# A decode layer on one core: wo loaded with eight rows to a partition, another selection of the attention output, and W_down's third quarter loaded in three parts

## The chip, the cores and the metric

The kernel runs on one core of a Trainium2 chip. The core has five engines with programs of their own: TensorE (PE; PEld is its loading of weights), VectorE (DVE), ScalarE (ACT), GpSimd (POOL) and SyncE (SP). They meet through semaphores. Data come from the chip's memory (HBM) by DMA: an engine, here nearly always SP, issues a transfer, and 16 DMA engines carry it out in the order of SP's queue. The metric is the device time of one execution in microseconds (us), lower is better. The kernel before takes 384.69 us, the median of three runs (384.29 to 384.77).

## The reference

One decode step (four sequences, one token each, model width 576) of a transformer layer: normalization, attention over a window of a cache, projection, residual, normalization, a gated feed-forward block, residual. All tensors are bf16.

```python
def _A_ref(x, k_cache, v_cache, wq, wo):       # 32 query heads, 16 kv heads, head size 128
    W = min(4096, max(256, Sk // 4))           # Sk = 16384: the last 4096 positions
    q = (x @ wq).reshape(B, Sq, Hq, Dh).transpose(0, 2, 1, 3)
    k = jnp.repeat(k_cache[:, :, Sk - W:, :], rep, axis=1)   # rep = 2
    v = jnp.repeat(v_cache[:, :, Sk - W:, :], rep, axis=1)
    scores = jnp.einsum("bhqd,bhkd->bhqk", q, k) * (Dh ** -0.5)
    o = jnp.einsum("bhqk,bhkd->bhqd", _softmax(scores), v)
    return o.transpose(0, 2, 1, 3).reshape(B, Sq, Hq * Dh) @ wo      # wo: 4096 x 576

def _B_ref(x, W_gate, W_up, W_down):           # 576 x 4608, 576 x 4608, 4608 x 576
    gate = jnp.einsum("bsd,df->bsf", x, W_gate)
    up = jnp.einsum("bsd,df->bsf", x, W_up)
    gate = gate * (gate > 0)
    return jnp.einsum("bsf,fd->bsd", gate * up, W_down)

h = x + _A_ref(_layernorm(x), A_k_cache, A_v_cache, A_wq, A_wo)
h2 = h + _B_ref(_layernorm(h), B_W_gate, B_W_up, B_W_down)
```

Nearly all bytes are the cache's windows: 64 loads of 2 MB, and some 25 MB of weights.

## The kernel before

The program is written once per engine (`prog_sync`, `prog_pool`, `prog_act`, `prog_dve`, `prog_pe`). A small class, `Sched`, counts what each engine has done: an operation may carry a name, and another that lists the name in `deps` waits for its engine's counter. So the order on each engine is the order in which the code is written, and a wait holds back all that stands behind it on the same engine. Every DMA has a semaphore of its own kind; `land(name)` is the wait for its landing.

*Memory and the load queue.* One buffer, `pool`, has eight slots of 2 MB: four for K, four for V. `add` (lines 195 to 206) puts a transfer on a list and notes which earlier users of those bytes must be done. SP walks through that list (`prog_sync`, line 263): wq, then K and V in turn (a "duo" is two kv heads of one sequence, 4096 positions each), then, into slots that have come free, the four loads of wo (`("wo", g)`, g = 0 to 3), W_gate and W_up (`wg0`, `wu0`, `wg1`, `wu1` of 256 rows each, then `wg4`, `wu4` of the last 64), and W_down (`("wd", k)`). W_down's 4608 rows are 36 chunks of 128 rows; it is loaded as `WD` says (line 247): three quarters of nine chunks each, then 3, 3, 2 and 1 chunks. In a quarter, each partition holds nine rows that are neighbours in memory. The W_down loads overwrite the bytes of wo, so the first of them waits for `ATTN`, the last matmul of the output projection.

*Attention.* Per duo VectorE transposes K (`tr`), TensorE multiplies by the query (`qk`), and per batch of four duos VectorE takes maxima, ScalarE the exponentials, VectorE transposes the probabilities, TensorE multiplies by V (`pv`). `ext` and `norm` bring the result to `oT_all`: 128 partitions (a head's 128 features) by 32 heads by 4 sequences.

*The output projection (lines 587 to 603).* The product with wo sums over 4096 rows (head and feature). A load of wo covers 1024 rows, which is eight heads. Before the change a partition holds two pieces of four neighbouring rows (4608 bytes each): row 512 q + 4 p + e of the load lies in partition p. So the attention output must be rearranged to fit: for each e and each head's place h4 in a group of four, one matmul with a strided piece of the identity picks the features 4 k + e of eight heads and puts them on 32 partitions (16 matmuls, 32 columns each, `OSEL`); VectorE copies the result as bf16 to `oX` (`D_OX`, line 464). Then 160 matmuls, each with a 128 x 128 (or 128 x 64) piece of wo as the weights and four columns of `oX`, add up into one PSUM bank (`WOB`).

*After it.* VectorE adds the residual (`H1`, `H2`), TensorE sums for mean and variance (`STAT`), VectorE and ScalarE normalize (`S1` to `N2`), and TensorE runs gate and up: 40 matmuls for each of four 128-feature slices, each slice's weights waited for, and then those of the last 64 features. ScalarE and VectorE form max(gate, 0) x up and transpose it (`HHT`), and TensorE multiplies by W_down: per chunk two matmuls of 288 columns, one for each half of the output, on different partitions. Each transfer of W_down is waited for before its first chunk. ScalarE and VectorE copy the two halves to `out_sb`, and SP stores it.

Of the kernel before, what the change touches and what calls it, by code (L numbers as in the profile page):

```python
# [21 lines left out]
FC = F // 128  # L22
DC = 5
NDUO = B * KVH // 2
NB = 4
NBATCH = NDUO // NB
# [7 lines left out]
ROW = 4608  # L34
GU0 = 24064
NWO = 4
# [66 lines left out]
def bass_sequential_preLN__sliding_block_cached__glu_gated_reglu__decode_kernel(  # L103
# [12 lines left out]
    with ExitStack() as es:  # L116
        cnt = [0]

        def sb(name, shape, dt):
            return es.enter_context(nc.sbuf_tensor(name, shape, dt))  # L120

        pool = sb("pool", [128, (NKS + NVS) * DUO], BF16)
        kT = sb("kT", [128, NKT, DUO // 4], FP32)
        ident_b = sb("ident_b", [128, 128], BF16)
# [11 lines left out]
        x4 = sb("x4", [64, B], BF16)  # L136
        dup = sb("dup", [64, 128], BF16)
        par = sb("par", [128, 2], FP32)
        oX = sb("oX", [128, 4, H // 4, B], BF16)
        xT = sb("xT", [128, DC, B], FP32)  # L140
        qT_sb = sb("qT_sb", [128, H * B], BF16)
        qrep = sb("qrep", [128, 4, H * B], BF16)
# [12 lines left out]
        P = sb("P", [128, T * 32], FP32)  # L155
        probT = sb("probT", [128, T, 32], FP32)
# [4 lines left out]
        oT_all = sb("oT_all", [128, H, B], BF16)  # L161
# [6 lines left out]
        gate_sb = P[:, 0:NG * JW].rearrange("p (g j f) -> p g j f", g=NG, j=JJ)  # L168
        hh = P[:, NG * JW:NG * JW + NG * JW // 2].bitcast(BF16).rearrange("p (g j f) -> p g j f", g=NG, j=JJ)
        hhT = probT[:, 0:FC // 2, :].bitcast(BF16).rearrange("p f b -> p (f b)")[:, 0:FC * 32].rearrange("p (f b) -> p f b", b=32)  # L170
        out_sb = sb("out_sb", [B, D], BF16)

        sc = es.enter_context(nc.psum_tensor("sc", [128, 2048], FP32))
        pb = [sc[:, i * 512:(i + 1) * 512] for i in range(4)]
        pb += [es.enter_context(nc.psum_tensor(f"pb{i}", [128, 512], FP32))[:, :] for i in range(4, 8)]
        PVB, OB, QB, QR, TPB = 4, 6, 6, 3, 7
        OSB, WOB, STB, SUB, DNB = 0, 1, 2, 5, 4


        GUB = ((0, 3, 6), (7, 1, 2))  # L180
# [7 lines left out]
        S = Sched()  # L188
# [4 lines left out]
        at = {}  # L193
# [30 lines left out]
        for c in range(2):  # L224
            add(("wq", c), f"wq{c}", NKS * DUO + 2 * c * HQ, 2 * HQ, "QMM",
                lambda e, o, c=c: e.dma_start(out=o, in_=A_wq[c * 256:(c + 1) * 256, :].rearrange("(p u) n -> p (u n)", u=2)))
# [6 lines left out]
                add_V(m - VLEAD)  # L233
        for g in range(NWO):
            add(("wo", g), f"wo{g}", g * ROW, ROW, "ATTN",
                lambda e, o, g=g: e.dma_start(out=o.rearrange("p (q x) -> p q x", q=2),
                                              in_=A_wo[g * 1024:(g + 1) * 1024, :].rearrange("(q p e) n -> p q (e n)", q=2, e=4)))
        for c in range(2):
            for k, (kind, W) in enumerate((("wg", B_W_gate), ("wu", B_W_up))):
                add((kind, c), f"{kind}{c}", GU0 + (4 * c + 2 * k) * ROW, 2 * F, None,  # L240
                    lambda e, o, c=c, W=W: e.dma_start(out=o, in_=W[c * 256:(c + 1) * 256, :].rearrange("(p u) n -> p (u n)", u=2)))
        for u, (kind, W) in enumerate((("wg", B_W_gate), ("wu", B_W_up))):
            add((kind, 4), f"{kind}4", GU0 + 8 * ROW + u * HALF, HALF, None,
                lambda e, o, W=W: e.dma_start(out=o, in_=W[512:576, :].rearrange("r (u n) -> (r u) n", u=2)))

        wd_sb = pool[:, 0:FC * D].rearrange("p (g x) -> p g x", g=NG)
        WD = [(0, 9), (9, 18), (18, 27), (27, 30), (30, 33), (33, 35), (35, 36)]
        for k, (f0, f1) in enumerate(WD):
            g0, j0 = divmod(f0, JJ)
            g1, nj = (f1 // JJ, JJ) if f1 - f0 >= JJ else (g0 + 1, f1 - f0)  # L250
# [2 lines left out]
                                  out=wd_sb[:, g0:g1, j0 * D:(j0 + nj) * D],  # L253
                                  in_=B_W_down[g0 * 128 * JJ:g1 * 128 * JJ, :].rearrange("(g p j) n -> p g (j n)", p=128, j=JJ)[:, :, j0 * D:(j0 + nj) * D])))

        def feat(c):
            return slice(c // 2 * 256 + c % 2, c // 2 * 256 + c % 2 + 255, 2) if c < 4 else slice(512, D)
# [104 lines left out]
        def prog_dve(S):  # L362
            v = "vector"
            S.op(v, lambda e: e.tensor_scalar(out=st1[:, 2:3], in0=st1[:, 0:1], scalar1=1.0 / D, scalar2=None, op0=ALU.mult),
                 deps=["A_SUM"], name="D1")
# [4 lines left out]
                 deps=["D3"], name="D_VARC")  # L370
            for ce in range(4):
                S.op(v, lambda e, ce=ce: e.tensor_copy(  # L372
                    out=sel[:, ce, :, :],
                    in_=bass.AP(tensor=ident_b, offset=64 * (ce // 2) + ce % 2, ap=[[128, 128], [0, 4], [2, 32]])),
                    deps=["IDB"], name=f"SEL{ce}")
            S.op(v, lambda e: e.tensor_copy(out=dup[:, :].rearrange("p (r u) -> p r u", u=2),
                                            in_=bass.AP(tensor=ident_b, offset=0, ap=[[128, 64], [1, 64], [0, 2]])), name="DUP")
            S.op(v, lambda e: e.tensor_reduce(out=par[:, :], in_=ident_b[:, :].rearrange("p (r u) -> p u r", u=2), axis=AX.X, op=ALU.add),
                 name="PAR2")
            for x in range(2):  # L380
# [3 lines left out]
                                              axis=AX.X, op=ALU.add), name="M0")  # L384
            S.op(v, lambda e: e.tensor_scalar(out=mask[:, 1, :], in0=mask[:, 0, :], scalar1=2 * BIG, scalar2=-BIG, op0=ALU.mult, op1=ALU.add),
                 deps=["M0"], name="M1")
            S.op(v, lambda e: e.tensor_scalar(out=mask[:, 2, :], in0=mask[:, 0, :], scalar1=-2 * BIG, scalar2=BIG, op0=ALU.mult, op1=ALU.add),
                 name="M2")
            for u in range(2):
                S.op(v, lambda e, u=u: e.tensor_reduce(out=rsel[:, u:u + 1], in_=mask[:, 1, :].rearrange("p (r s h) -> p s r h", s=2, h=2)[:, u, :, :],  # L390
                                                       axis=AX.XY, op=ALU.max), deps=["M1"] if u == 0 else [], name=f"RSEL{u}")
# [4 lines left out]
                 deps=["TP1"], name="D_XNT0")  # L396
# [3 lines left out]
            for u in range(2):  # L400
                S.op(v, lambda e, u=u: e.tensor_scalar(out=xn4[:, u, :], in0=pb[STB][:, 0:B], scalar1=par[:, u:u + 1], scalar2=None, op0=ALU.mult),
                     deps=["XDUP", "PAR2"], name=f"XN4{u}")
# [41 lines left out]
            for i in range(2 * NDUO):  # L444
                tr(i)
                if i == 0:
# [3 lines left out]
                                                    in_=bass.AP(tensor=ident_f, offset=0, ap=[[128, 128], [4, 4], [32, NB], [1, 4]])),  # L450
                         deps=["IDF"], name="SELT")
                n, pos = divmod(i, 2 * NB)
# [5 lines left out]
                if i >= 29 and (i - 29) % KVH == 0:  # L458
                    norm((i - 29) // KVH)
            trp(NBATCH - 1)  # L460
            for b in range(B):
                if 29 + KVH * b >= 2 * NDUO:
                    norm(b)
            S.op(v, lambda e: e.tensor_copy(out=oX[:, :, :, :].rearrange("p e q b -> p (e q b)"), in_=pb[OSB][:, 0:H * B]),
                 deps=["OSEL"], name="D_OX")

            S.op(v, lambda e: e.tensor_tensor(out=R_sb[:, 0, 0:4, :], in0=pb[WOB][:, 0:16].rearrange("p (c b) -> p c b", b=B),
                                              in1=xT[:, 0:4, :], op=ALU.add), deps=["ATTN", "R0", "D_XT"], name="H1")
            S.op(v, lambda e: e.tensor_tensor(out=R_sb[0:64, 0, 4, :], in0=pb[WOB][0:64, 16:20], in1=xT[0:64, 4, :], op=ALU.add), name="H2")
            S.op(v, lambda e: e.tensor_tensor(out=R_sb[:, 1, :, :], in0=R_sb[:, 0, :, :], in1=R_sb[:, 0, :, :], op=ALU.mult),  # L470
                 deps=["H2"], name="D_R")
            S.op(v, lambda e: e.tensor_reduce(out=st2[:, 0:8], in_=pb[SUB][:, 320:360].rearrange("p (s c b) -> p s b c", s=2, c=DC, b=B),
                                              axis=AX.X, op=ALU.add), deps=["STAT"], name="S1")
# [5 lines left out]
                 deps=["S4"], name="D_VARC2")  # L479
# [21 lines left out]
        def prog_pe(S):  # L501
            t = "tensor"

            def mm(o, l, r, start, stop, deps=(), name=None, skip=False):
                S.op(t, lambda e: e.matmul(o, lhsT=l, rhs=r, start=start, stop=stop, skip_group_check=skip),  # L505
                     deps=deps, name=name, signal=name is not None)
# [16 lines left out]
            s = at[("wq", 4)]  # L523
# [60 lines left out]
                    pv(i - PVLAG)  # L584
            ext(NBATCH - 1)

            for e_ in range(4):
                for h4 in range(4):
                    mm(pb[OSB][32 * h4:32 * h4 + 32, e_ * 32:(e_ + 1) * 32], ident_b[:, e_:128:4],
                       oT_all[:, :, :].rearrange("p (q h) b -> p h q b", h=4)[:, h4, :, :], True, True,  # L590
                       deps=[("NORM", b) for b in range(B)] if e_ == 0 and h4 == 0 else [],
                       name="OSEL" if e_ == 3 and h4 == 3 else None)
            for g in range(NWO):
                wv = pool[:, at[("wo", g)]:at[("wo", g)] + ROW].rearrange("p (q e n) -> p q e n", q=2, e=4)
                deps = [land(("wo", g))] + (["D_OX"] if g == 0 else [])
                for n in range(DC):
                    w = 128 if n < 4 else 64
                    for q in range(2):
                        for e_ in range(4):
                            last = g == NWO - 1 and n == DC - 1 and q == 1 and e_ == 3  # L600
                            mm(pb[WOB][0:w, n * B:(n + 1) * B], wv[:, q, e_, feat(n)], oX[:, e_, 2 * g + q, :],
                               g == 0 and n == 0 and q == 0 and e_ == 0, last, deps=deps, name="ATTN" if last else None, skip=True)
                            deps = []
            mm(pb[SUB][:, 320:360], ones_f[:, :], R_sb[:, :, :, :], True, True, deps=["D_R"], name="STAT")
            mm(pb[SUB][:, 400:400 + B], dup[:, :], hnT[0:64, 4, 0:B], True, True, deps=["N2"], name="HDUP")

# [90 lines left out]
```

## Time and profile before

| | |
|---|---|
| median of three runs | 384.69 us (384.29 to 384.77) |
| the profiled execution | 384.86 us, span 383.1 us, mean granted clock 0.887 |
| TensorE, VectorE, ScalarE, GpSimd busy | 76%, 53%, 14%, 2% of the span |
| loaded | 159.6 MB, 417 GB/s over the span |
| last W_down matmul ends, output copied, end of the span | 380.84, 381.3, 383.1 us |

The span runs from the first to the last instruction of the program; 1.8 us of the execution's time lie around it. In the profile's rows "L505" is the helper that issues every matmul, so matmuls are told apart by the names of their tiles: `sc` and `pb` are PSUM, `pool` holds all loaded data. "SPq" is SP issuing a DMA. "x36" counts instructions merged in a row, and the two numbers ahead are the start and the length in us. The arrow names what ended the idle time. In the rows of DMA issues the last number is the time from the issue to the landing on the last of the 16 DMA engines. The matmuls' lengths overlap, since they are pipelined.

### The profile page before, as it was taken

Reading aid. Unit: us, or ns where it says so; the run is one execution under the profiler, and the core shown is the slowest. Engines: PE = TensorE matmul, PEld = TensorE weight load, DVE = VectorE, ACT = ScalarE, POOL = GpSimd, SP = SyncE. Lnnn points to the kernel's source line nnn. Section 1 sums busy time; section 2 is a strip of 40 time slices with the busy share of each in tenths; the row PEclk is TensorE's granted clock in tenths of the full one; section 3 lists DMA queues with packets and bytes.
Section 4 is the critical chain, followed back from the end, with each engine's and each line's share of the span. In section 5 each row is a group of like instructions: output and inputs, shape, how many; then the busy total and the mean of one; then the engine's idle time right before and its main releaser. Section 6 shows DMA issues by size and latency. Waiting matters only on the chain.

```text
span 383.1 us, 3926 instructions
## 1 busy us (share of the span) xinstructions
PE 289.2 (76%) x1705; PEld 125.5 (33%) x1720; DVE 202.4 (53%) x189; ACT 53.5 (14%) x129; POOL 8.2 (2%) x22
## 2 busy tenths in 40 slices
PE   0069559977997799769966996799579887982465
PEld 0054113322432243224322432243224333371242
DVE  0369799269436954684477547744865441011030
ACT  4021040021102110211021102110310021010020
POOL 4100000000000000000000000000000000000000
PEclk9999958995999799989998999899989996965675
DMA  8999999999999999999999999999999999999994
GB/s 315 426 424 429 428 428 429 425 429 426 427 431 426 424 431 429 423 431 429 421 433 429 423 429 429 426 429 429 424 431 429 423 430 426 407 428 429 414 425 161
DMA packets 12641, 159.84 MB, mean 417 GB/s; under 512 B 1352, under 2 KB 1488, under 8 KB 3280
## 3 DMA queue, kind: packets, MB, share of 16 engines
q1 hardware_dynamic: 12616, 159.59, 98.5%
q8 instruction: 13, 0.21, 0.2%
q14 instruction: 4, 0.03, 0.0%
q10 hardware_dynamic: 8, 0.00, 0.0%
HBM read 159.58 MB, written 0.00 MB: 417 GB/s over the span
## 4 chain that ended last, share of the span: by engine, by line
PE 50%; DVE 18%; issue 15%; DMA 8%; ACT 6%; POOL 1%; SPq 0%; POOLq 0%
PE sc L505 26%; PE pb L505 24%; DMA pool<-in_B_W_down_dram 8%; DVE kT L411 6%; ACT P L340 5%; DVE probT L430 4%; DVE rmx L414 4%; POOL bcm L291 1%; DVE bias L426 0%; SPq L252 0%; DVE rowsum L435 0%; DVE pmax L417 0%; DVE t L422 0%; DVE bmin L424 0%; DVE sel L372 0%
## 5 line engine op out<-in xcount | busy, mean ns | idle before, releaser
L411 DVE STREAM_TRANSPOSE kT<-pool 128x2048 f32<-128x2048 f32 x64 | 144.7, 2293 | 51.0 <-DMA pool<-in_A_k_cache_dram 40.5
L505 PE MATMUL sc<-kT,qz 128*128 128x512 bf16 x497 | 134.7, 425 | 48.1 <-DVE kT L411 44.6
L505 PE MATMUL pb<-pool,prob 128*16 128x512 bf16 x512 | 117.6, 389 | 0.0
L505 PEld LDWEIGHTS sc<-kT,qz 128*128 128x128 bf16 x512 | 49.5, 103 | 129.7 <-DVE kT L411 53.5
L505 PEld LDWEIGHTS pb<-pool,prob 128*16 128x16 bf16 x512 | 43.8, 91 | 71.5 <-issue 17.7
L340 ACT ACTIVATE P<-sc,bias 128x512 f32<-128x512 f32 x32 | 22.2, 718 | 176.1 <-DVE bias L426 176.1
L414 DVE TENSOR_REDUCE rmx<-sc 128x2 f32<-128x2048 f32 x8 | 18.3, 2292 | 38.3 <-PE sc L505 38.3
L430 DVE STREAM_TRANSPOSE probT<-P 128x2048 f32<-128x2048 f32 x8 | 18.5, 2311 | 7.9 <-ACT P L340 7.9
L512 PE MATMUL pb<-ident_b,xn_bf 4*128 4x4 bf16 (+1 forms) x5 | 0.4, 175 | 19.4 <-ACT xn_bf L304 19.4
L325 ACT COPY cp<-pb 128x512 f32<-128x512 f32 x8 | 4.7, 585 | 68.8 <-PE pb L505 68.8
L505 PE MATMUL pb<-selT,cp 128*128 128x16 f32 x64 | 8.7, 269 | 4.3 <-ACT cp L325 4.3
L492 DVE TENSOR_TENSOR P<-pb,P 128x288 bf16<-128x288 f32 (+1 forms) x2 | 0.8, 402 | 21.1 <-PE pb L505 21.1
L439 DVE RECIPROCAL rs_sb<-pb 128x32 f32<-128x32 f32 x4 | 1.4, 342 | 19.8 <-PE pb L505 19.8
L505 PEld LDWEIGHTS pb<-selT,cp 128*128 128x128 f32 x64 | 9.0, 208 | 6.3 <-ACT cp L325 5.3
L347 ACT CAST prob<-probT 128x1024 bf16<-128x1024 f32 x8 | 8.4, 1045 | 19.0 <-DVE rs L433 19.0
L505 PE MATMUL pb<-pool,hnT 128*32 128x288 bf16 (+1 forms) x48 | 4.0, 406 | 9.3 <-DMA pool<-in_B_W_up_dram 9.3
L505 PE MATMUL pb<-pool,probT 128*4 128x288 bf16 x72 | 7.0, 364 | 4.9 <-DMA pool<-in_B_W_down_dram 4.9
L291 POOL PARTITION_ALL_REDUCE bcm<-pmax x8 | 3.1, 388 | 291.6 <-DVE pmax L417 291.6
L318 ACT COPY qz<-qrep 32x64 bf16<-32x64 bf16 x32 | 7.8, 245 | 7.3 <-DVE qrep L448 7.0
L505 PE MATMUL sc<-pool,hnT 128*32 128x288 bf16 (+2 forms) x112 | 6.8, 367 | 0.9 <-DMA pool<-in_B_W_gate_dram 0.9
L372 DVE COPY sel<-ident_b 128x128 bf16<-128x128 bf16 x4 | 1.1, 450 | 10.7 <-POOL ident_b L276 10.7
L512 PEld LDWEIGHTS pb<-ident_b,xn_bf 4*128 4x128 bf16 (+1 forms) x5 | 0.3, 106 | 19.4 <-ACT xn_bf L304 19.4
(103 smaller groups left out, 86.6 us busy)
## 6 DMA issues: line engine op xcount, KB each, us to landing
pool<-in_A_k_cache_dram SPq DMA_DIRECT2D x32, 2048.0 KB, 27.0
pool<-in_A_v_cache_dram SPq DMA_DIRECT2D x32, 2048.0 KB, 24.9
pool<-in_A_wo_dram SPq DMA_DIRECT2D x4, 1152.0 KB, 21.6
pool<-in_B_W_gate_dram SPq DMA_DIRECT2D x2, 2304.0 KB, 24.7
pool<-in_B_W_up_dram SPq DMA_DIRECT2D x2, 2304.0 KB, 27.3
pool<-in_A_wq_dram SPq DMA_DIRECT2D x2, 2048.0 KB, 10.1
pool<-in_B_W_down_dram SPq DMA_DIRECT2D x3, 1296.0 KB, 29.0
pool<-in_B_W_down_dram SPq DMA_DIRECT2D x2, 432.0 KB, 31.9
```

The lines of the kernel that those rows point to most:

```text
L291: S.op(g, lambda e, n=n: e.partition_all_reduce(bcm[:, n % 2, :], pmax[:, n % 2, :], 128, bass_isa.ReduceOp.max), deps=deps, name=("PAR", n))
L318: S.op(a, lambda e, src=src, dst=dst: e.copy(out=dst, in_=src), deps=deps, name=("QZ", n) if g == 3 else None, signal=g == 3)
L325: S.op(a, lambda e: e.copy(out=cp[:, n % 2, :], in_=pb[PVB + n % 2]), deps=deps, name=("CP", n))
L340: S.op(a, lambda e, n=n, th=th, u=u: e.activation(out=P[:, th * 1024 + u:(th + 1) * 1024:2], in_=sc[:, th * 1024 + u:(th + 1) * 1024:2], f ...
L347: S.op(a, lambda e, n=n: e.copy(out=prob[:, n % 2, :, :, :], in_=probT[:, :, 0:NHB].rearrange("p t (r x) -> p r t x", x=4)), deps=deps, na ...
L372: S.op(v, lambda e, ce=ce: e.tensor_copy(out=sel[:, ce, :, :], in_=bass.AP(tensor=ident_b, offset=64 * (ce // 2) + ce % 2, ap=[[128, 128], ...
L411: S.op(v, lambda e: e.transpose(out=dst, in_=src), deps=deps, name=("TR", i))
L414: S.op(v, lambda e: e.tensor_reduce(out=rmx[:, n % 2, :], in_=sc[:, :].rearrange("p (x u) -> p u x", u=2), axis=AX.X, op=ALU.max), deps=[( ...
L430: S.op(v, lambda e: e.transpose(out=probT[:, :, :].rearrange("p t j -> p (t j)"), in_=P[:, :]), deps=[("EXP", n, 1)] + ([("CMP", n - 1)] i ...
L439: S.op(v, lambda e: e.reciprocal(out=rs_sb[:, b, :], in_=pb[OB][:, 64 + b * H:64 + (b + 1) * H]), deps=[("SUM", b)], name=("RS", b))
L492: S.op(v, lambda e, x=x: e.tensor_tensor(out=hh[:, x[0], :, x[1]:x[2]], in0=part(1, x, "j f"), in1=gate_sb[:, x[0], :, x[1]:x[2]], op=ALU. ...
L505: S.op(t, lambda e: e.matmul(o, lhsT=l, rhs=r, start=start, stop=stop, skip_group_check=skip), deps=deps, name=name, signal=name is not None)
```

## The change

1. A load of wo gives each partition eight neighbouring rows (9216 bytes in one piece): row 8 p + e of the load lies in partition p.
2. The attention output is rearranged to fit. A 128 x 1024 pattern `S8` is made once from the identity: for each e it has 128 columns that pick feature 8 k + e, repeated for the eight heads. Eight matmuls of 128 columns (all heads and sequences at once) write 1024 columns of PSUM; VectorE multiplies by the mask `mask8`, which keeps in partition 16 s + k only the columns of the heads whose place in their load is s, sums over the eight places, and copies to `oX`. The mask is made at the start of VectorE's program, `S8` after the last transposition of the probabilities. The selection's PSUM is two banks wide, so the projection's bank moves from 1 to 3. `S8`, the product and its sums live in parts of `probT` and `P` that are free by then.
3. W_down's third quarter (chunks 18 to 27) is loaded as three parts of three chunks, each waited for by itself: nine transfers instead of seven.

```diff
-        oX = sb("oX", [128, 4, H // 4, B], BF16)
+        oX = sb("oX", [128, 8, NWO, B], BF16)
+        mask8 = sb("mask8", [128, 8], FP32)
...
+        S8 = probT[:, FC // 2:FC // 2 + 16, :].bitcast(BF16).rearrange("p f b -> p (f b)")
+        oM = P[:, 0:1024]
+        oS = P[:, 1024:1024 + H * B]
...
-        OSB, WOB, STB, SUB, DNB = 0, 1, 2, 5, 4
+        OSB, WOB, STB, SUB, DNB = 0, 3, 2, 5, 4
...
-                lambda e, o, g=g: e.dma_start(out=o.rearrange("p (q x) -> p q x", q=2),
-                                              in_=A_wo[g * 1024:(g + 1) * 1024, :].rearrange("(q p e) n -> p q (e n)", q=2, e=4)))
+                lambda e, o, g=g: e.dma_start(out=o,
+                                              in_=A_wo[g * 1024:(g + 1) * 1024, :].rearrange("(p e) n -> p (e n)", e=8)))
...
-        WD = [(0, 9), (9, 18), (18, 27), (27, 30), (30, 33), (33, 35), (35, 36)]
+        WD = [(0, 9), (9, 18), (18, 21), (21, 24), (24, 27), (27, 30), (30, 33), (33, 35), (35, 36)]
...
+            S.op(v, lambda e: e.tensor_reduce(out=mask8[:, :], in_=ident_b[:, :].rearrange("p (s k) -> p s k", s=8), axis=AX.X, op=ALU.add), name="MASK8")
...
+            S.op(v, lambda e: e.tensor_copy(out=S8.rearrange("p (e s k) -> p e s k", e=8, s=8),
+                                            in_=bass.AP(tensor=ident_b, offset=0, ap=[[128, 128], [1, 8], [0, 8], [8, 16]])),
+                 deps=[("CMP", NBATCH - 1)], name="S8")
...
-            S.op(v, lambda e: e.tensor_copy(out=oX[:, :, :, :].rearrange("p e q b -> p (e q b)"), in_=pb[OSB][:, 0:H * B]),
-                 deps=["OSEL"], name="D_OX")
+            S.op(v, lambda e: e.tensor_tensor(out=oM.rearrange("p (x s b) -> p x s b", s=8, b=B),
+                                              in0=sc[:, 0:1024].rearrange("p (x s b) -> p x s b", s=8, b=B),
+                                              in1=bass.AP(tensor=mask8, offset=0, ap=[[8, 128], [0, 32], [1, 8], [0, B]]), op=ALU.mult),
+                 deps=["OSEL", "MASK8"], name="D_OM")
+            S.op(v, lambda e: e.tensor_reduce(out=oS.rearrange("p (x b) -> p x b", b=B),
+                                              in_=oM.rearrange("p (x s b) -> p x b s", s=8, b=B), axis=AX.X, op=ALU.add),
+                 deps=["D_OM"], name="D_OS")
+            S.op(v, lambda e: e.tensor_copy(out=oX[:, :, :, :].rearrange("p e g b -> p (e g b)"), in_=oS), deps=["D_OS"], name="D_OX")
...
-            for e_ in range(4):
-                for h4 in range(4):
-                    mm(pb[OSB][32 * h4:32 * h4 + 32, e_ * 32:(e_ + 1) * 32], ident_b[:, e_:128:4],
-                       oT_all[:, :, :].rearrange("p (q h) b -> p h q b", h=4)[:, h4, :, :], True, True,
+            for e_ in range(8):
+                mm(sc[:, e_ * 128:(e_ + 1) * 128], S8[:, e_ * 128:(e_ + 1) * 128], oT_all[:, :, :].rearrange("p h b -> p (h b)"), True, True,
+                   deps=[("NORM", b) for b in range(B)] + ["S8"] if e_ == 0 else [], name="OSEL" if e_ == 7 else None)
...
+                    for e_ in range(8):
+                        last = g == NWO - 1 and n == DC - 1 and e_ == 7
+                        mm(pb[WOB][0:w, n * B:(n + 1) * B], wv[:, e_, feat(n)], oX[:, e_, g, :],
+                           g == 0 and n == 0 and e_ == 0, last, deps=deps, name="ATTN" if last else None, skip=True)
```

More of the change, by code (lines that the diff above doesn't have):

```diff
@@ L585, in prog_pe @@
             ext(NBATCH - 1)
-            for e_ in range(4):
-                for h4 in range(4):
-                    mm(pb[OSB][32 * h4:32 * h4 + 32, e_ * 32:(e_ + 1) * 32], ident_b[:, e_:128:4],
-                       oT_all[:, :, :].rearrange("p (q h) b -> p h q b", h=4)[:, h4, :, :], True, True,
-                       deps=[("NORM", b) for b in range(B)] if e_ == 0 and h4 == 0 else [],
-                       name="OSEL" if e_ == 3 and h4 == 3 else None)
+            for e_ in range(8):
+                mm(sc[:, e_ * 128:(e_ + 1) * 128], S8[:, e_ * 128:(e_ + 1) * 128], oT_all[:, :, :].rearrange("p h b -> p (h b)"), True, True,
+                   deps=[("NORM", b) for b in range(B)] + ["S8"] if e_ == 0 else [], name="OSEL" if e_ == 7 else None)
             for g in range(NWO):
-                wv = pool[:, at[("wo", g)]:at[("wo", g)] + ROW].rearrange("p (q e n) -> p q e n", q=2, e=4)
+                wv = pool[:, at[("wo", g)]:at[("wo", g)] + ROW].rearrange("p (e n) -> p e n", e=8)
                 deps = [land(("wo", g))] + (["D_OX"] if g == 0 else [])
@@ L597, in prog_pe @@
                     w = 128 if n < 4 else 64
[L598 to L603, printed above, removed]
+                    for e_ in range(8):
+                        last = g == NWO - 1 and n == DC - 1 and e_ == 7
+                        mm(pb[WOB][0:w, n * B:(n + 1) * B], wv[:, e_, feat(n)], oX[:, e_, g, :],
+                           g == 0 and n == 0 and e_ == 0, last, deps=deps, name="ATTN" if last else None, skip=True)
+                        deps = []
             mm(pb[SUB][:, 320:360], ones_f[:, :], R_sb[:, :, :, :], True, True, deps=["D_R"], name="STAT")
```

## The prediction

> **What bounds the kernel now.** I read the page first, then the chain that ended last, then the timeline of the last 50 us, the DMA queue's issues one by one with their time to landing, and last the clock by windows. The page's slices of the DMA engines:
>
> ```profile
> DMA  8999999999999999999999999999999999999994
> GB/s 315 426 424 429 428 428 429 425 429 426 427 431 426 424 431 429 423 431 429 421 433 429 423 429 429 426 429 429 424 431 429 423 430 426 407 428 429 414 425 161
> ```
>
> The 16 DMA engines are busy in every slice but the first and the last, at some 428 GB/s. No engine bounds the middle: a stage costs time only if it makes the DMA queue run dry, or if it lies behind the last landing. Slice 35 (407 GB/s) is where wo is loaded. The end of the chain:
>
> ```profile
> 345.28 31.00 DMA pool<-in_B_W_down_dram
> 376.31 4.50 PE pb L505 x36
> 380.84 0.45 DVE out_sb L498
> ```
>
> After 345.28 the chain is one DMA, W_down's third quarter, and then 36 matmuls that wait for nothing more. The issues of that quarter and of the four small parts behind it:
>
> ```profile
> 345.28 0.43 SPq L252 DMA_DIRECT2D pool<-in_B_W_down_dram  x1
> 345.75 0.43 SPq L252 DMA_DIRECT2D pool<-in_B_W_down_dram  x1
> 346.23 7.89 SPq L252 DMA_DIRECT2D pool<-in_B_W_down_dram  x1
> 354.16 4.77 SPq L252 DMA_DIRECT2D pool<-in_B_W_down_dram  x1
> 358.97 2.77 SPq L252 DMA_DIRECT2D pool<-in_B_W_down_dram  x1
> pool<-in_B_W_down_dram SPq DMA_DIRECT2D x1, 1296.0 KB, 31.0
> pool<-in_B_W_down_dram SPq DMA_DIRECT2D x1, 432.0 KB, 31.6
> pool<-in_B_W_down_dram SPq DMA_DIRECT2D x1, 432.0 KB, 32.1
> pool<-in_B_W_down_dram SPq DMA_DIRECT2D x1, 288.0 KB, 24.9
> pool<-in_B_W_down_dram SPq DMA_DIRECT2D x1, 144.0 KB, 20.5
> ```
>
> Issue plus time to landing: the quarter lands at 376.28, the parts at 377.35, 378.33, 379.06 and 379.47. So the last byte is there at 379.47, but the last matmul ends at 380.84: at the end TensorE, not the DMA, is late. Why, the windows show (columns: window, length, TensorE, weight loads, VectorE, ScalarE, GpSimd, granted clock, DMA share, GB/s):
>
> ```profile
> 370.10:371.40 1.30, 1.27 (x18) 0.71 (x18) 1.27 (x4) 0.00 (x0) 0.00 (x0) 1.00 0.93 383
> 373.20:374.50 1.30, 1.27 (x18) 0.70 (x18) 0.00 (x0) 0.00 (x0) 0.00 (x0) 1.00 0.95 392
> 376.30:380.80 4.50, 4.48 (x36) 2.19 (x36) 0.00 (x0) 0.00 (x0) 0.00 (x0) 0.50 0.27 104
> ```
>
> The first two quarters take 1.27 us for 18 matmuls at clock 1.00, the last 36 take 4.48 us at 0.50. Two matmuls (the two output halves) start together, so a pair comes every 0.12 us at full and 0.24 us at half clock: 18 pairs x 0.24 = 4.3, and 0.2 more for the last to come through.
>
> **The change, part by part.** Times are those of the profiled execution: 384.86 us, of which 383.1 are the span. It stands 0.17 above the median of the three runs shown (384.69).
>
> *W_down's third quarter in three parts, on TensorE.* Its 9 pairs start in threes as the parts land, instead of all after 376.31. At half clock three pairs take 0.72 us, and the 432 KB parts land 1.0 to 1.07 us apart (rows above): TensorE catches up before each next landing. With the landings as before: the 288 KB part at 379.06 gives two pairs, at 379.10 and 379.34; the last pair starts at 379.58 and ends 0.45 later (a matmul's length in that stretch), at 380.03. That is 0.8 us before 380.84. At full clock the last pair starts with its landing, 379.51, and ends 0.33 later: 1.0 us gained. I take 0.8, the half clock, which this execution had there. Bounds: 0 (TensorE was not late in other executions, below) and 1.0.
>
> *The same, on the queue.* The extra rows are 3456 bytes instead of 10368. The nearest rows are the two 432 KB parts: 1.07 and 0.98 us each, mean 1.03 to 1.05, against a third of a quarter's 3.1 (370.04, 373.12 and 376.28 by the same reckoning), 1.03. So +0.0 to +0.04 each, three times: +0.06, bounds 0 and 0.12. Two more issues stand in SP's queue ahead of the output's. The 5th issue already sat 7.89 us for a place, the 6th 4.77, the 7th 2.77; places come as older transfers land, and wg4 and wu4 land before W_down's first quarter starts (370.04 less 3.1 = 366.9). Two more places are there by about 367, and their bytes are due after 378. Nothing.
>
> The Trainium skill, in "DMA: Bandwidth & Descriptors", section "Rules for kernel authors", asks for at least 1 MiB per DMA for full bandwidth, which speaks against cutting 1.3 MB in three (its section on the anatomy of a DMA gives GpSimd's path a fixed 2.0 us, so an estimate of +4 us for two more). The 432 KB rows above, 1.03 us apart, do not show it.
>
> *wo with 9216 bytes in a row instead of two times 4608.* The four loads were issued at 315.33, 315.98, 316.49 and 317.00 and took:
>
> ```profile
> pool<-in_A_wo_dram SPq DMA_DIRECT2D x1, 1152.0 KB, 18.2
> pool<-in_A_wo_dram SPq DMA_DIRECT2D x1, 1152.0 KB, 20.4
> pool<-in_A_wo_dram SPq DMA_DIRECT2D x1, 1152.0 KB, 22.7
> pool<-in_A_wo_dram SPq DMA_DIRECT2D x1, 1152.0 KB, 25.0
> ```
>
> They land at 333.53, 336.38, 339.19 and 342.00: 2.82 to 2.85 us for 1.18 MB, 414 to 418 GB/s. W_down's quarters with rows of 10368 bytes take 3.1 for 1.33 MB, 428. At 427 a wo load takes 2.76. Gain 0.07 each, 0.3 in all; bounds 0 and 0.4 (four times 0.1). Everything behind on the queue comes that much earlier, the last landing too.
>
> *The selection.* Before: 16 small matmuls (0.31 us) and a cast (0.29) between the last normalization and wo. After: 8 matmuls of 128 columns, a multiplication of 1024 numbers out of PSUM, a sum over groups of 8, a cast. Matmuls: four of this shape took 0.61 for the query replication, so eight 0.6 more than the sixteen (bounds 0.2 and 0.9). Multiplication: 0.42 for 288 numbers in the gate's product, so 1.5. Sum: 2292 ns for 2048, so 1.15. Two more hand-offs, 0.05 each. Together +3.35; the dearest strided row, the selection copies at 450 ns for 128, would make the two operations 3.6 each and the whole +8.2; the lower bound is +1.5. It delays ATTN (343.74), and behind it:
>
> - SP's wait before W_down's first load, with all nine loads and the output queued. Its bytes are due at 366.9: 23 us of room.
> - the second normalization, VectorE's and ScalarE's ops up to 347.6, and the first gate matmuls. These run 1.15 us from 347.59 and then wait:
>
> ```profile
> 353.10 0.37 PE L505 MATMUL pb<-pool,hnT 128*32 128x216 bf16 x4 [4.36 <-DMA pool<-in_B_W_up_dram]
> 364.20 0.37 PE L505 MATMUL pb<-pool,hnT 128*32 128x216 bf16 x4 [4.93 <-DMA pool<-in_B_W_up_dram]
> ```
>
> With +3.35 they end at 352.1, before that landing (352.8 now). Beyond it 4.9 us of matmuls up to 358.0 and 0.8 from 358.6 must be done by 363.9: a delay up to 9.5 us costs nothing, and the upper bound is 8.2. So 0. wo itself keeps its 160 matmuls (5.92), now with all four loads there.
>
> *The rest.* The mask's sum is one more VectorE op of some 0.27 us (the parity sum, same input) ahead of the first projection; K's fifth load went out at 28.67 while some 33 us of loads were queued at the start, so 4 us of room cover it. The selection pattern's copy (at most 3.6 us by the dearest row) stands after the last transposition, where VectorE is idle from 317.1 to 336.3. The output projection's other PSUM bank is read before the gate's second write: nothing.
>
> Sum: -0.8 - 0.3 + 0.06 = -1.04: 383.8 for the profiled execution, 383.65 against the median. I say 383.8, since the plain runs gain less where TensorE was less late.
>
> **Rivals.**
>
> *Only the queue's part comes (0.2).* The half clock at the end is a matter of where the clock's steps fall: 1.00 up to 375.2, 0.50 after. If in the timed runs of before the step came later, the last 36 matmuls kept up with the landings and only 0.24 of the sum is left: 384.45. For it: the runs shown differ by 0.48 (384.29 to 384.77), and the bursts fill only 1.27 of 3.1 us, so there is little to choose. Against: 384.86 and two of three runs lie together. The Trainium skill, "TensorE: Matmul & The Clock Gate", Part 1, has the gate looked at in a free-running window of about 3.4 us; the steps here are 3.4 us or multiples of it apart, which agrees, and it makes the phase a matter of chance.
>
> *The last DMA engine gets later (0.1), the other side.* The last landing is that of the slowest of 16 engines: from 375.2 to 378.7 they are busy 0.61 of the time. They also fetch the program: 13 packets on the instruction queue, 0.2% of 16 engines' span, about 0.9 us each. The program of TensorE changes, and a packet that moves to the latest engine delays the last landing by 0.9; from the second on (+1.8) the kernel ends at 385.6, slower; one gives 384.7. For it: 16 engines, 13 packets, uneven. Against: up to 336 us TensorE's program is unchanged, and 10 of the 13 were fetched by then.
>
> *Small DMAs cost their completion (0.02).* If each of two more DMAs added a stretch of its own on the engines, the nearest row is the output's 4.5 KB: 0.35 to issue and 1.0 waited for. Two of these: 383.8 + 2.7 = 386.5. The 432 KB rows speak against it. (By the 2.0 us of the Trainium skill's page on DMA, named above, it would be 387.8.)
>
> *The selection is over 9.5 us longer (0.03).* Then wu1's matmuls start late and the end follows one for one: at 12 us, 386.3.
>
> **How the numbers follow.** 0.2% of 384.69 is 0.77 us, about what a measurement of this kernel can tell: faster is under 383.92, slower above 385.46. The likeliest case (0.65) lies between 383.4 and 384.15 (both clocks, wo's bounds); 0.61 of it I put below 383.92. Same is the other 0.04, the queue's case (0.2) and one packet (0.06): 0.30. Slower is the second packet (0.04), the small DMAs (0.02) and the selection (0.03): 0.09. The range 383.3 to 384.8 takes in the queue's case and one packet.
>
> **What would show it.** In the profile after: between 374 and 380 four stretches of TensorE that each wait for W_down instead of one of 36 matmuls, and the last landing followed within 0.7 us by the output's copies; the wo loads 2.76 us apart; ATTN near 347 and the wait for the first W_up still there (over 0.3 us). The prediction is wrong if TensorE's last 36 matmuls still wait once, if wo's landings keep 2.85 us, or if the last landing comes after 379.5.

## The result, and the profile after

The changed kernel takes 383.84 us (22 runs, 383.62 to 384.04) beside 384.69 for the kernel before (22 runs by now, 383.73 to 387.05). The ratio is 0.998, 95% interval 0.9973 to 0.9987: 0.85 us faster, and the changed kernel's times lie much closer together. The profiled execution took 383.99 us, its span 382.2.

The end of the chain of the changed kernel, to be held against that of before (start and length in us):

```profile
358.78 19.51 DMA pool<-in_B_W_down_dram
378.33 1.62 PE pb L520 x12
379.98 0.45 DVE out_sb L513
```

The DMA at the end of the chain is no longer W_down's third quarter but the second of the small parts behind it, and 12 matmuls follow it instead of 36. The timeline of TensorE from the second quarter on:

```profile
373.06 1.64 PE L520 MATMUL pb<-pool,probT 128*4 128x288 bf16 x24 [1.85 <-DMA pool<-in_B_W_down_dram]
375.19 0.53 PE L520 MATMUL pb<-pool,probT 128*4 128x288 bf16 x6 [0.49 <-DMA pool<-in_B_W_down_dram]
376.22 0.53 PE L520 MATMUL pb<-pool,probT 128*4 128x288 bf16 x6 [0.49 <-DMA pool<-in_B_W_down_dram]
377.28 0.53 PE L520 MATMUL pb<-pool,probT 128*4 128x288 bf16 x6 [0.53 <-DMA pool<-in_B_W_down_dram]
378.33 1.60 PE L520 MATMUL pb<-pool,probT 128*4 128x288 bf16 x12 [0.52 <-DMA pool<-in_B_W_down_dram]
```

Each group of six has an idle stretch before it that ends with a landing: TensorE has caught up every time. The 24 are the second quarter's 18 and the first part's six. The last issue and its time to landing:

```profile
362.83 1.61 SPq L256 DMA_DIRECT2D pool<-in_B_W_down_dram  x1
pool<-in_B_W_down_dram SPq DMA_DIRECT2D x1, 144.0 KB, 16.5
```

These rows give the time to landing to 0.1 us. The DMA engines' own records are finer: the last landing is at 379.36, 0.62 us before the copies at 379.98; before the change it was 379.45 and 380.84, so 1.40. Of the 0.86 us by which the last copies come earlier, 0.78 are TensorE's lateness and 0.08 the landing's. The granted clock was 0.50 at the very end here too (same columns as in the windows of before):

```profile
375.20:377.90 2.70, 1.59 (x18) 0.52 (x18) 0.00 (x0) 0.00 (x0) 0.00 (x0) 1.00 0.67 263
378.30:380.00 1.70, 1.60 (x12) 0.41 (x12) 0.02 (x1) 0.02 (x1) 0.00 (x0) 0.50 0.09 33
```

wo's four loads (issued at 315.13, 315.77, 316.24 and 316.72) and the selection, from the DMA issues and the timeline:

```profile
pool<-in_A_wo_dram SPq DMA_DIRECT2D x1, 1152.0 KB, 18.1
pool<-in_A_wo_dram SPq DMA_DIRECT2D x1, 1152.0 KB, 20.5
pool<-in_A_wo_dram SPq DMA_DIRECT2D x1, 1152.0 KB, 22.8
pool<-in_A_wo_dram SPq DMA_DIRECT2D x1, 1152.0 KB, 25.1
...
336.79 0.81 PE L520 MATMUL sc<-oT_all,probT 128*128 128x128 bf16 x8 [0.72 <-DVE oT_all L446]
337.64 1.23 DVE L473 TENSOR_TENSOR P<-sc,mask 128x1024 f32<-128x1024 f32 x1 [0.90 <-PE sc L520]
338.90 1.97 DVE L477 TENSOR_REDUCE P<-P 128x128 f32<-128x1024 f32 x1
340.90 0.23 DVE L480 CAST oX<-P 128x128 bf16<-128x128 f32 x1
347.22 17.23 SPq L256 DMA_DIRECT2D pool<-in_B_W_down_dram  x9
352.90 0.37 PE L520 MATMUL pb<-pool,hnT 128*32 128x216 bf16 x4 [1.09 <-DMA pool<-in_B_W_up_dram]
```

By the DMA engines' records the loads of wo are 2.77 to 2.78 us apart on the first engine to finish, close to the 2.76 that was forecast. But a load has landed when the last engine is done, and these landings are 3.06, 2.79 and 2.79 us apart: 8.64 from the first to the fourth, where the kernel before had 8.53. So one sign of the prediction, that wo's landings come closer together, did not show itself.

ATTN, and with it W_down's first issue, comes at 347.22, 3.48 us later than before. The wait for the first W_up has shrunk from 4.36 to 1.09 us, but it is still there, so the delay is gone from that point on.

### The profile page after: what moved, and what is told of

Read it like the earlier page. It is cut to its first block, busy times and chain, and to the rows that moved or that the text cites. A ratio compares the mean times of both kernels' runs of the same rounds, so it can differ in the third digit from the quotient of the medians.

```text
span 382.2 us, 3916 instructions
## 1 busy us (share of the span) xinstructions
PE 287.7 (75%) x1697; PEld 124.5 (33%) x1712; DVE 206.5 (54%) x193; ACT 53.5 (14%) x129; POOL 8.2 (2%) x22
## 4 chain that ended last, share of the span: by engine, by line
PE 50%; DVE 18%; issue 16%; ACT 6%; DMA 5%; SPq 3%; POOL 1%; POOLq 0%
PE sc L520 27%; PE pb L520 23%; DVE kT L416 6%; ACT P L344 5%; DMA pool<-in_B_W_down_dram 5%; DVE probT L435 4%; DVE rmx L419 4%; SPq L256 3%; POOL bcm L295 1%; DVE P L477 1%; DVE bias L431 0%; DVE rowsum L440 0%; DVE pmax L422 0%; DVE t L427 0%; DVE bmin L429 0%
## 5 line engine op out<-in xcount | busy, mean ns | idle before, releaser
L520 PE MATMUL sc<-kT,qz 128*128 128x512 bf16 x497 | 133.1, 422 | 48.4 <-DVE kT L416 45.1
L520 PE MATMUL pb<-pool,probT 128*4 128x288 bf16 x72 | 6.1, 310 | 5.4 <-DMA pool<-in_B_W_down_dram 5.4
L520 PE MATMUL sc<-oX,pool 128*128 128x4 bf16 (+1 forms) x160 | 5.9, 172 | 3.7 <-DVE oX L480 3.7
L520 PEld LDWEIGHTS sc<-oX,pool 128*128 128x128 bf16 (+1 forms) x160 | 5.8, 114 | 4.0 <-issue 3.9
```

## The experiments

Three theories were to be told apart. A: TensorE, at half clock, is what is late at the end, and the split takes that away. B: the gain is wo's longer rows, which bring all later landings forward. C, on the selection: its delay is free only up to 9.5 us, as the prediction had it, or for longer. The runs were made in three groups, each on one chip with the kernel before beside it: it took 384.49 in the first (35 runs), 384.60 in the second (27) and 384.56 in the third (35).

### The split alone (first group, and again in the third)

```diff
-        WD = [(0, 9), (9, 18), (18, 27), (27, 30), (30, 33), (33, 35), (35, 36)]
+        WD = [(0, 9), (9, 18), (18, 21), (21, 24), (24, 27), (27, 30), (30, 33), (33, 35), (35, 36)]
```

wo and the selection as before.

> Theory A (TensorE at half clock is what is late at the end, and the split takes that away): nearly the whole gain, 0.7 to 0.8 us, so 383.9 to 384.0 beside 384.7; in the trace the third quarter's matmuls come in three groups that each wait, and the output's copies begin some 0.6 us after the last landing instead of 1.4. Rival B (the gain comes from wo's longer rows, which bring every later landing forward): 0.1 or less, 384.6 to 384.8.

Measured: 384.07 (383.90 to 384.43), ratio 0.9989 (0.9980 to 0.9998), 0.42 under the kernel before. The trace shows the groups that each wait, as in the changed kernel, and the copies begin 0.62 us after the last landing:

```profile
375.31 0.53 PE L505 MATMUL pb<-pool,probT 128*4 128x288 bf16 x6 [0.53 <-DMA pool<-in_B_W_down_dram]
376.33 0.53 PE L505 MATMUL pb<-pool,probT 128*4 128x288 bf16 x6 [0.49 <-DMA pool<-in_B_W_down_dram]
...
378.46 1.60 PE L505 MATMUL pb<-pool,probT 128*4 128x288 bf16 x12 [0.54 <-DMA pool<-in_B_W_down_dram]
```

The gain is about half of what theory A said. Its interval begins at 0.08 us, so this run alone does not quite exclude B's 0.1. The second time, in the third group:

> The split in three alone, as the second base: 383.95 to 384.1. If splitting and keeping the clock up take away the same lateness, it lies within 0.2 of the warm kernel.

384.03 (383.82 to 384.32), ratio 0.9988 (0.9979 to 0.9996), 0.53 under before, with an interval that begins at 0.15. So the split is worth 0.4 to 0.5 us in plain executions, not the 0.8 of one profiled pair, and more than B allows.

### wo's rows and the selection alone (first group)

The changed kernel with `WD` as it was before:

```diff
-        WD = [(0, 9), (9, 18), (18, 21), (21, 24), (24, 27), (27, 30), (30, 33), (33, 35), (35, 36)]
+        WD = [(0, 9), (9, 18), (18, 27), (27, 30), (30, 33), (33, 35), (35, 36)]
```

> Theory A: wo's landings 2.77 us apart instead of 2.85, so up to 0.3 us on each DMA engine, but the last landing is the slowest engine's and moved by only 0.07 in the changed kernel; the last 36 matmuls still wait once. Gain 0.1 to 0.3: 384.4 to 384.6. The selection's 3.5 us more are hidden behind the wait for the first W_up. Rival B: gain 0.6 or more, 384.1 or less.

Measured: 384.50, ratio 0.9994 (0.9984 to 1.0004): no gain to be told by the median. But the twelve times are in two heaps: 383.45, 383.51, 383.68, 383.88, one at 384.16, and seven from 384.44 to 384.74, 1.0 us apart by their means. The profiled execution took 384.62, and its windows show where the upper heap comes from:

```profile
373.40:376.40 3.00, 2.31 (x18) 0.99 (x18) 0.00 (x0) 0.00 (x0) 0.00 (x0) 0.50 0.93 377
376.50:380.00 3.50, 3.50 (x30) 1.86 (x32) 0.00 (x0) 0.00 (x0) 0.00 (x0) 0.50 0.27 103
380.00:380.60 0.60, 0.56 (x10) 0.17 (x4) 0.00 (x0) 0.00 (x0) 0.00 (x0) 0.99 0.00 0
```

The half clock came at 373.2 here, and the last 36 matmuls ran without a break to 380.6, 1.0 us past the last landing (379.63). That in the lower heap the half clock fell elsewhere was not seen directly, since no execution of it was profiled; the kernels with fillers, below, bear on it.

### The clock kept up, nothing split (first group, and again in the third)

```diff
+            FILL = (6, 6, 0, 0, 0, 0, 0)
             for k, (f0, f1) in enumerate(WD):
...
+                for _ in range(FILL[k]):
+                    mm(pb[SUB], ident_b[:, :], qrep[:, :, :].rearrange("p c x -> p (c x)"), True, True)
```

The kernel before with matmuls of no use behind the first two quarters of W_down, into a bank that nobody reads any more.

> The kernel before with six filler matmuls of 512 columns on TensorE behind each of the first two quarters of W_down, into a PSUM bank nobody reads any more; nothing split. Theory A with the half clock as its cause: the granted clock stays at 1.00 past 376, the 36 matmuls take some 2.2 us and keep up with the landings, and the end comes 0.9 us earlier without any split: 383.8. If the clock has no part in it (the single wait for the whole quarter is enough to be late): 384.6 to 384.8.

Measured: 383.89 (383.66 to 384.15 and one at 386.01), ratio 0.9986 (0.9976 to 0.9997), 0.60 under before. Windows and timeline of the end:

```profile
374.50:376.30 1.80, 1.49 (x8) 0.51 (x6) 0.00 (x0) 0.00 (x0) 0.00 (x0) 1.00 0.90 362
376.40:378.60 2.20, 1.70 (x26) 0.95 (x28) 0.00 (x0) 0.00 (x0) 0.00 (x0) 1.00 0.44 173
...
376.42 1.64 PE L505 MATMUL pb<-pool,probT 128*4 128x288 bf16 x24 [0.44 <-DMA pool<-in_B_W_down_dram]
378.54 0.53 PE L505 MATMUL pb<-pool,probT 128*4 128x288 bf16 x6 [0.48 <-DMA pool<-in_B_W_down_dram]
379.25 0.65 PE L505 MATMUL pb<-pool,probT 128*4 128x288 bf16 x6 [0.17 <-DMA pool<-in_B_W_down_dram]
```

The single wait for the whole quarter is still there, at 376.42. But the clock stays at 1.00, the third quarter and the first small part take 1.64 us, and the later parts are waited for. TensorE is late no more: the copies begin 0.37 us after the last landing. So the half clock was the cause, and the order of the waits alone was not. Nor was the half clock alone, since with the split and 0.50 at the end the copies begin 0.62 us after the last landing instead of 1.40. It took both. The second time:

> The kernel before with the fillers, as the base of the comparison: 383.85 to 383.95, 0.6 to 0.8 under before.

383.93 (383.74 to 384.29), ratio 0.9985 (0.9976 to 0.9994): 0.63 under before, and within 0.1 of the split alone beside it (384.03). Both edits take away the same lateness.

### wo's rows, with the clock out of the way (third group)

> wo's longer rows and the new selection, the third quarter in one piece, and the fillers of the warm kernel (six behind each of the first two quarters), so that TensorE's clock plays no part. The difference to the warm kernel of this group is wo's rows alone. If each DMA engine's 0.3 us reach the end: 0.25 to 0.35 under it, 383.5 to 383.6. If the slowest engine's lag eats them, as in the one profiled pair (0.07): 383.8.

The changed kernel with `WD` as before and `FILL = (6, 6, 0, 0, 0, 0, 0)` as in the last experiment. Measured: 383.81 (383.58 to 384.04), 0.12 under the warm kernel without wo's rows (383.93).

> The changed kernel beside the split alone: the difference is wo's rows and the selection. If 0.3 us reach the end: 383.65 to 383.8, 0.25 to 0.4 under the split alone. If not: within 0.15 of it.

The changed kernel itself, in the same group: 383.82 (383.53 to 383.99 and one at 385.74; ratio 0.9987, 0.9975 to 1.0), 0.21 under the split alone (384.03). So wo's rows are worth 0.1 to 0.2 us at the end, between the two answers, and theory B's 0.6 does not come. Each of these four kernels' times spread over some 0.5 us, so either difference alone is hardly clear of the noise; the landings agree with them. In the second group the changed kernel was run beside others:

> The changed kernel, unaltered, beside the others of this group. Theory A with two parts: the split alone gave 0.42 of 384.49 and wo's rows alone 0.0 by the median (0.06% by the ratio); if the parts simply add, this is 384.0 to 384.1. If the two help each other (the split makes the end follow the last landing in every execution, and only then do wo's earlier landings count), it is 383.8 to 383.9.

383.69 (383.55 to 383.88) beside 384.60, ratio 0.9978 (0.9968 to 0.9988). Against the split's and wo's parts from the third group (0.53 and 0.21) this is a little more than their sum, by 0.2 us, on another chip; whether the parts help each other is not settled by that.

The trace also tells when each DMA engine finishes a transfer. On the first engine to finish, the time from the last V to the last load of wo is 11.40 to 11.43 us in the six profiled executions with the old rows and 11.12 to 11.16 in the eight with the new: 0.28 us less, every time. The last landing of all lies at 379.42 to 379.57 in the five with the old rows and the quarter in one piece or three, and at 379.26 to 379.63 in the eight with the new, on average 0.12 earlier. So each engine gains its 0.3, and the slowest one, which counts, loses some of it again.

The program's own loads (13 packets of 16 KiB in both profiles) are the likely reason. In each of these fourteen executions one of them, 1.06 to 1.11 us long, starts between 333.7 and 334.5 us, while wo is loaded. In each, one of the sixteen finishing times then falls back against the others by 1.5 to 1.7 us: in wo's second load, or in the third in the two executions where the packet came last (334.40 and 334.48). In the changed kernel it goes from 1.9 to 3.4 us behind the first engine, where the slowest until then had been 3.1 behind, and the 0.28 us gained on wo are gone. In the kernel before, the engine only came level with the slowest (3.3). In the kernel with wo's rows alone it went from 2.3 to 3.8, and its last landing, 379.63, is the latest of the eight. No run moved these packets, so this is read from the traces and not tried.

### The selection's two operations done five times over (second group)

```diff
+            for r_ in range(5):
...
-                 deps=["OSEL", "MASK8"], name="D_OM")
+                     deps=["OSEL", "MASK8"] if not r_ else [f"D_OS{r_ - 1}"], name=f"D_OM{r_}")
...
-                 deps=["D_OM"], name="D_OS")
+                     deps=[f"D_OM{r_}"], name=f"D_OS{r_}")
```

> The changed kernel with the selection's multiplication and sum done five times over, so ATTN comes near 360.1 instead of 347.2, 16.4 us later than before the change. By the prediction's own rule (beyond 9.5 us the end follows one for one): 383.8 + 6.9 = 390.7. Rival: TensorE stands idle for 1.8 of every 3.1 us while W_down lands, so gate and up that start late catch up before the third quarter: 383.6 to 384.0.

Measured: 383.79 (383.62 to 384.49), beside 383.69 for the changed kernel: nothing, with ATTN 16.4 us later than before the change. The timeline:

```profile
360.15 5.26 SPq L256 DMA_DIRECT2D pool<-in_B_W_down_dram  x9
363.59 0.91 PE L521 MATMUL sc<-pool,hnT 128*32 128x216 bf16 x16
...
373.50 3.47 PE L521 MATMUL pb<-pool,probT 128*4 128x288 bf16 x54 [1.23 <-DVE probT L511]
377.28 0.53 PE L521 MATMUL pb<-pool,probT 128*4 128x288 bf16 x6 [0.31 <-DMA pool<-in_B_W_down_dram]
378.34 0.53 PE L521 MATMUL pb<-pool,probT 128*4 128x288 bf16 x6 [0.53 <-DMA pool<-in_B_W_down_dram]
```

W_down's nine issues go out at 360.15 and its bytes still follow without a gap. Gate and up start at 363.59 and run through without a wait for a load. W_down's first 54 matmuls start at 373.50 instead of 369.94, all of them in one go at full clock, and at 377.28 TensorE waits for a landing again. The prediction's step that beyond a delay of 9.5 us the end follows one for one is wrong.

### Fillers on top of the change, too many and fewer

The changed kernel with the same filler loop:

```diff
+            FILL = (6, 6, 1, 1, 1, 1, 1, 0, 0)
```

> The changed kernel with the same fillers and one more behind each of the five 432 KB parts. Theory A: clock 1.00 to the end, so the last pair of matmuls ends 0.35 us after the last landing instead of 0.6: 383.6, 0.2 less than the changed kernel. Rival: where the clock drops all the same, a filler (0.43 us at half clock) stands ahead of the next part's matmuls and adds up to 0.4: 384.0 to 384.3.

Measured (first group): 384.17 (384.01 to 384.45), slower than the changed kernel in the other groups (medians 383.69 to 383.84), though the clock was 1.00 to the end. The rival had the price right and the reason wrong:

```profile
374.26 1.47 PE L520 MATMUL pb<-qrep,ident_b 128*128 128x512 bf16 x6
375.66 0.53 PE L520 MATMUL pb<-pool,probT 128*4 128x288 bf16 x6
376.13 0.39 PE L520 MATMUL pb<-qrep,ident_b 128*128 128x512 bf16 x1
376.45 0.53 PE L520 MATMUL pb<-pool,probT 128*4 128x288 bf16 x6
```

Six fillers behind the second quarter end at 375.66, 1.6 us after the first part has landed (374.08, from the DMA engines' records), and with one more filler per part (0.78 us for a part and a filler, against 1.05 between landings) TensorE does not make this up: no part is waited for, and the copies begin 0.76 us after the last landing.

> The changed kernel with fillers only where TensorE has room: three behind the first quarter of W_down, one behind each of the next three 432 KB parts and the first of the old ones. Theory A: clock 1.00 to the end without a backlog, the last pair ends 0.35 to 0.4 us after the last landing instead of 0.6: 383.6 to 383.7, 0.2 less than the changed kernel. If the half clock at the very end costs nothing: 383.8 to 383.9.

Against the fillers of the last run:

```diff
-            FILL = (6, 6, 1, 1, 1, 1, 1, 0, 0)
+            FILL = (3, 0, 1, 1, 1, 1, 0, 0, 0)
```

In the second group, with these, every part is waited for again and the clock is 1.00 to the end, but the time is 383.68 (383.58 to 383.80) beside 383.69 without fillers. The 0.2 us expected are not there. The changed kernel's own profile in that group suggests why: it had the half clock earlier, while the quarters land, and 1.00 at the end.

```profile
373.00:375.90 2.90, 2.90 (x26) 1.59 (x28) 0.00 (x0) 0.00 (x0) 0.00 (x0) 0.50 1.00 404
376.00:377.70 1.70, 1.30 (x20) 0.53 (x14) 0.00 (x0) 0.00 (x0) 0.00 (x0) 1.00 0.59 230
```

So the fillers had nothing to save in this execution. With the split it still matters where the half clock falls, but less. In the three profiled executions with the split and 0.50 at the very end (the changed kernel's first and third, and the first of the split alone) the copies begin 0.62 us after the last landing. In the eight with 1.00 there and no backlog, with the split or without it, they begin 0.37 us after it. Without split and fillers it was 1.40 and, with wo's rows, 0.98. No version was found that beats the changed kernel by more than the measurement can tell.

### The third quarter in nine parts (second group)

```diff
-        WD = [(0, 9), (9, 18), (18, 27), (27, 30), (30, 33), (33, 35), (35, 36)]
+        WD = [(0, 9), (9, 18), (18, 19), (19, 20), (20, 21), (21, 22), (22, 23), (23, 24), (24, 25), (25, 26), (26, 27), (27, 30), (30, 33), (33, 35), (35, 36)]
```

> The kernel before with the third quarter in nine parts of one chunk (144 KB, rows of 1152 bytes) instead of three. Theory A: each 144 KB part costs the queue some 0.03 us more than its bytes (0.37 against 0.344 for the last part), 0.2 to 0.25 in all, and TensorE is late no more: 384.2 to 384.3, between the split in three (384.07) and before. If small transfers cost their completion, 1.35 us each: over 390.

Measured: 384.22 (383.97 to 384.64), ratio 0.9994 (0.9985 to 1.0002). As expected of theory A: the 144 KB parts follow each other after 0.37 us, where their bytes at the quarters' rate need 0.34, the last landing is at 379.67 (379.49 and 379.57 with three parts), and finer parts give part of the gain back. Nothing like 1.35 us for each transfer is seen.

## Why the prediction was right, point by point

*The time* (383.8 predicted, 383.84 measured) came out by its steps, but two of them were larger than what plain executions show. The sum of the steps, 1.04, gives 383.65 against the median, 0.19 too low, and 383.82 for the profiled execution, which took 383.99. The higher of the two was stated because plain runs gain less; that reason held, but its size was not worked out, so that the median was met within 0.04 is in part luck.

*W_down's third quarter, on TensorE: 0.8 predicted.* The mechanism held: half clock, one long run of matmuls behind the landing, and the parts waited for one by one. In the profiled pair it is 0.78. In plain executions the split alone gave 0.42 and 0.53, since the kernel before is not late in all of them; this is the first rival's point, and it was right in part: the times of the kernel before, 383.73 to 385.12 (and one run at 387.05), spread far wider than the changed kernel's 383.62 to 384.04, which agrees with it.

*The same on the queue: 0.06.* Held. The last of the three parts lands 3.16 us behind the second quarter in the changed kernel, the whole third quarter 3.11 behind it before, and nine parts cost 0.1 to 0.2 more. The rule on 1 MiB per DMA that was quoted from the Trainium skill's page "DMA: Bandwidth & Descriptors" ("Rules for kernel authors") does not decide here: at 432 KB, queued behind one another, the three lose 0.05 us together.

*wo's rows: 0.3.* The size was right on each DMA engine (0.28), but only 0.12 to 0.21 of it reached the end, and 0.08 in the profiled pair. The step that failed is "everything behind on the queue comes that much earlier, the last landing too": the last landing is the slowest engine's, and that one did not keep its gain. By the prediction's own sign (landings that stay 2.85 apart, measured 2.88 on average) this step was wrong. It took 0.1 to 0.2 us off the sum.

*The selection: +3.35, hidden.* ATTN moved by 3.48; the last normalization ended 0.2 earlier, so the selection costs 3.7. The multiplication was dearer in the prediction than on the chip (1.5 against 1.23) and the sum cheaper (1.15 against 1.97): it takes 1.92 ns a number, the row it was priced by 1.12. Why was not tried. The cover was named rightly. Its depth was not: the step "a delay up to 9.5 us costs nothing" and the rival that starts there counted TensorE's work up to the last W_up as fixed in place, and 16.4 us cost nothing.

*The clock's rule.* The page "TensorE: Matmul & The Clock Gate" of the Trainium skill (Part 1) has a free-running window of about 3.4 us. The executions profiled here agree: the half clock came at 375.2, 378.0, 373.2 and 372.5 in different runs, and every stretch of it that ends before the span does is 3.41 us long or a whole multiple of that (6.8, 20.5).

*The other rivals.* The last landing did not get later, so the slowest DMA engine did not turn the result. But the rival's price was too low: an engine falls back by 1.5 to 1.7 us where 0.9 was taken for one packet of the program, and this is the likely place of the missing part of wo's gain. Small transfers at 1.35 us each are ruled out by the nine parts.

## What to carry to other kernels

Where the DMA engines are busy throughout, look at the stretch behind the last landing: what counts there is how much work waits for one late transfer, and at which clock it runs. Cutting a late transfer into parts makes the end follow the last landing within 0.37 to 0.62 us, whatever the clock does, which is worth more in the spread than in the best run. A stage ahead of idle stretches can be late by more than the first of them: here 16.4 us cost nothing, where the first wait was 4.4. What the limit is was not tried.

## What the runs showed of the hardware that was not expected

- One program's times can fall into two heaps (383.45 to 383.88 and 384.44 to 384.74 in eleven of twelve runs of the kernel with wo's rows alone). The profiled execution of the upper heap had the half clock over the last matmuls; with the clock kept up by fillers, the same kernel's twelve times lie in one heap, 383.58 to 384.04.
- Bursts of 1.27 us every 3.1 us did not always keep the clock up; with six matmuls of 512 columns more in each gap (1.47 us) it stayed at 1.00 in all profiled executions, 0.60 and 0.63 us faster without any other edit.
- Rows of 9216 bytes instead of 4608 make a 1.18 MB load 0.07 us shorter on each DMA engine (0.28 for four), and the last of the 16 engines, 3.2 to 3.8 us behind the first at the end, kept less than that.
- The 16 engines start the kernel before within 1.0 us of each other. While a packet of the program is fetched, one of them falls back by 1.5 to 1.7 us and stays behind: seen in all fourteen profiled executions while wo is loaded.
